# Pieces of the last layer's weight conversion tied to single chunks of the experts, and 20 instead of 16 of them in the last layer's first group

## The chip, the core and the metric

The kernel runs on one core of a Trainium2 chip. The core has five engines that run side by side and wait for each other by semaphores: PE (TensorE, matmuls; its weight loads are counted apart as PEld), DVE (VectorE), ACT (ScalarE), POOL (GpSimd) and SP (SyncE, which here only issues DMAs). Each engine takes its instructions strictly in the order in which they were put down for it. The metric is the device time of one execution in microseconds (us), lower is better. Before the change the median of 3 runs is 927.39 us (926.62 to 931.57).

## The reference: what is computed

Three layers one after the other, all in float32 at the outside.

```
attention:  state += beta * k_n (v - state k_n)^T,  y_t = q_t state     32 heads, 768 steps, 48 wide
experts:    logits = x w_gate + bias[modality];  e = argmax
            out = gate * (relu(x w1[e]) w2[e])                          3072 tokens, 384 -> 1024 -> 384, 8 experts
last layer: h = x w_in;  out = (h * sigmoid(h)) w_out                   3072 tokens, 384 -> 2048 -> 384
```

The weights `w_in` and `w_out` of the last layer come in as float64 (two 32-bit words per number). The kernel itself turns them into pairs of 32-bit numbers, a high part and a low part, since each product of the last layer is made of three matmuls: high by high, high by low, low by high. This conversion is what the change moves.

## The kernel before

**The experts.** Tokens are sorted by expert and handled in passes. The first five passes (0 to 4) take 2 blocks of 128 tokens each and overlap with the end of the attention layer and with the router, which works out on DVE where each token goes. Their order on every engine comes from a planner (class `Order`, `Experts.plan`), with a job for each step and a rank. Passes 0 to 2 use the weights as they are in the second product; passes 3 and 4 (`passes=(3, 4)`) split all weights into high and low parts. Then come four passes of 4 blocks each (`Experts.regular`, `Experts.slot`). Every pass goes through 8 chunks of the hidden width: `first` multiplies tokens by a chunk of w1 (9 matmuls, tile `ph` or `bank`), ACT makes the rectified high part and DVE the low part of the result (L1393 and L1397 into `hhl` in passes 3 and 4, L1474 and L1475 into `pairs` in the later ones), and `second` multiplies it by a chunk of w2 into `po` or `poe`. The high and low parts of the weights come from ACT (L1354, L1262) and DVE (L1357, L1263), out of buffers `raw` that SP fills by DMA. The 32 chunks of the four later passes are counted 40 to 71. In the last of these passes, after its first chunk, stands a test (`extra`, L1557 and L1558): every engine reads a number and branches around passes that are hardly ever needed.

**The conversion.** `Parts64` turns one part of the weights (12 parts `ri` of 128x512 of w_in, 16 parts `ro` of 128x384 of w_out). A part has a DMA, two DVE instructions that take bits out of the high words (L1586, L1587), one on ACT (L1588), then three on DVE (L1590, L1591, L1593), one on ACT that writes the high part (L1594) and one on DVE that writes the low part (L1595). `Ffn.chain` cuts the parts into pieces: piece 2i finishes part i (L1590 to L1595), piece 2i+1 asks for the load of part i+2 and begins part i+1 (L1586 to L1588). Two raw buffers are there, so a load of part i+2 waits until part i is read. The first 20 parts give 40 pieces that go with the experts, the last 8 parts (`ro8` to `ro15`) give 16 pieces that go with the first group of the last layer.

**What sets the order around the change.** The pieces are not jobs of the planner. They are traced in the loop over chunks 40 to 71, and a scheduler that simulates the program then puts every instruction in the place where it expects its operands. In the loop nothing ties a piece to its chunk, so a piece may be placed earlier than the chunk at which it was traced. In the last layer each piece is tied: `tc.issue_after(x)` puts what is traced under it behind instruction x, on x's engine.

**The last layer.** `Ffn.group` handles 512 tokens, in 16 steps f: `first(f)` (9 matmuls into `fph`, L1705), on ACT and DVE the activation and its high and low parts (L1708 to L1714), and `second(f-1)` into `fpo` (L1723). `tokens` loads the next group's tokens (`fy`) and transposes them on DVE.

Of the kernel before, what the change touches and what calls it, by code (L numbers as in the profile page):

```python
# [12 lines left out]
AF = mybir.ActivationFunctionType  # L13
ALU = mybir.AluOpType
# [12 lines left out]
        o=566.7, w=-158.5, wc=-114, up=-190.2, uc=85.6, ps=-63.1, sc2=420.4, py=136, Y=-126, out=290, xt=-319.5,  # L27
# [24 lines left out]
        xc2=-308.8, xc3=-299, xc4=-108.6, xc5=-186.8, gt0=-119.9, gt1=249, gt2=-393.6, gt3=-396.9, gt4=-275.9,  # L52
        gt5=-409.8,
    ), half=106.1,
    ex=-155.5, n0=40, npre=40, tok=70,
)


class Order:
# [137 lines left out]
    def emit(self, tc, pulse, close):  # L197

        nc = tc.nc
        traced, last = nc.cur_bb.bb.instructions, {}  # L200
        info = mybir.DependencyInfo(mybir.DependencyClass.NoSync, mybir.DependencyReason.DATA)
        wait = mybir.DependencyInfo(mybir.DependencyClass.Sync, mybir.DependencyReason.DATA)
        made = {}
        line = [(j["start"], 0, n, j) for n, j in enumerate(self.line)]
        final = max((x for x in line if x[3]["key"][0] not in self.LATER), key=lambda x: x[:3])[3]
        line += [(x, 1, n, k) for n, (x, k) in enumerate(self.pulses())]
        for _, kind, _, j in sorted(line, key=lambda x: x[:3]):
            at = len(traced)
            if kind:
                x = pulse()  # L210
                if j is not None:
                    tc.add_manual_dep(x, made[j], wait, reason="pulse")
            else:
                j["fn"]()
                if len(traced) > at:
                    made[j["key"]] = traced[-1].name
            new = {}
            for x in traced[at:]:
                new.setdefault(x.engine, []).append(x)
            for e, xs in new.items():  # L220
                for x in xs:
                    if e in last:
                        tc.add_manual_dep(x, last[e].name, info, reason="order")
                last[e] = xs[-1]
            if j is final:
                close()
# [10 lines left out]
class Attention:  # L237
# [501 lines left out]
    def run(self, router, experts, close):  # L739
        nc, P = self.nc, self.pools  # L740
        dense = router.ones
        room = self.ranks[:, 256:512].rearrange("p (a b) -> p a b", b=128)
        self.dense, self.rows = dense, [sized(x, [128, 16, 32]) for x in experts.po]

        def pulse():
            twice = [
                nc.tensor.matmul(room, dense, dense[:, None, :].to_broadcast([128, 2, 128]), start=True, stop=True).ins
                for _ in range(2)
            ]
            return twice[0]  # L750

        o = self.plan(router, experts)
        o.solve()
        o.emit(self.tc, pulse, close)


class Router:
# [454 lines left out]
class Experts:  # L1212
# [249 lines left out]
    def slot(self, n, blocks, x, po, fetch=None, nxt=None, last=False, alone=False, between=None):  # L1462

        nc, P, g, m = self.nc, self.P, self.r.groups[n], len(blocks)
        F, b0 = self.F, blocks[0]
        xh, xl = x

        def first(c, h1, l1):  # L1470
            ph = self.bank([128, 128 * m], f"ph{n}_{b0}_{c}")
            self.first(ph, h1, l1, xh, xl)
            hh, hl = self.take("hh", m), self.take("hl", m)
            nc.scalar.activation(hh, ph, AF.Relu)  # L1474
            nc.vector.scalar_tensor_tensor(hl, ph, 0.0, hh, op0=ALU.max, op1=ALU.subtract)  # L1475
            return hh, hl

        prev = None
        for c in range(F):
            w = self.split(0, c)  # L1480
            if between is not None and c == 1:
                between()
            cur = first(c, *w)
            w = self.split(1, c)
            if fetch is not None and c % 2:
                for part in range(2):
                    fetch(part, c - 1, c + 1)
            if prev is not None:
                self.second(c - 1, po, *prev)
            prev = cur + w  # L1490
            if alone:
                self.second(c, po, *prev)
                prev = None
            if nxt is not None:
                nxt(c)
            yield
        if prev is not None:
            self.second(F - 1, po, *prev)
        for t, o in enumerate(blocks):
            ysb = self.take("ysb", 4 * n)  # L1500
            if t % 2:
                nc.vector.tensor_scalar(ysb, po[t], g["gate"][:, o : o + 1], None, op0=ALU.mult)
            else:
                nc.scalar.mul(ysb, po[t], g["gate"][:, o : o + 1])
            self.scatter(n, o, ysb, last)
# [93 lines left out]
class Ffn:  # L1599
# [91 lines left out]
    def group(self, g, x, nxt, fill=()):  # L1691
        nc, P = self.nc, self.P
# [41 lines left out]
        prev = None  # L1734
        for f in range(16):
            cur = first(f)
            for fn in fill[f : f + 1]:
                with self.tc.issue_after(self.marks[0]), self.tc.issue_after(self.marks[1]):
                    fn()
            if f == 8 and nxt is not None:  # L1740
                self.x = self.tokens(nxt)
            if prev is not None and (f < 15 or nxt is not None):
                second(f - 1, *prev)
            if f < 15 or nxt is not None:
                prev = cur
# [71 lines left out]
@with_exitstack  # L1817
def fused_kernel(ctx: ExitStack, tc, kt, qb, kd, vd, beta, mod, w_gate, bias, w1, w2, w_in, w_out, out):
    nc = tc.nc

    def pool(stack, name, bufs=1, **kw):
        return stack.enter_context(tc.tile_pool(name=name, bufs=bufs, **kw))

    N, D = out.shape
    P = {
        "dram": pool(ctx, "dram", space=DRAM), "cc": pool(ctx, "cc"),
        "pa": pool(ctx, "pa", 5, space=PSUM), "pm": pool(ctx, "pm", 3, space=PSUM),
    }
    ident = P["cc"].tile([128, 128], F32, name="ident")

    xs = P["dram"].tile([N, D], F32, name="xs")
    ys = P["dram"].tile([N, D], F32, name="ys")
    P["rc"] = pool(ctx, "rc")

    with ExitStack() as moe:
        for name in ("ar", "ld"):
            P[name] = pool(moe, name, side="right")
        rank = ExitStack()
        P["rs"] = pool(rank, "rs", side="right")
        with ExitStack() as att:  # L1840
            for name in ("ac", "ln"):
                P[name] = pool(att, name)
            for name in ("sm", "y"):
                P[name] = pool(att, name, 2)
            attn = Attention(tc, ident, P, kt, qb, kd, vd, beta, xs)
            router = Router(tc, ident, P, attn.B, attn.T, w_gate, bias, mod, attn)
            experts = Experts(tc, ident, P, router, w1, w2, xs, ys, attn.bank)
            f = []

            def close():  # L1850
                att.close()
                P["fw"], P["f0"] = pool(ctx, "fw"), pool(ctx, "f0")
                f.append(Ffn(tc, ident, P, w_in, w_out, ys, out))
                add_pair_buffers(experts.bufs, P["fw"], f[0])
                P["rb"] = Views([P["fw"].tile([128, 6144], F32, tag=tag, name="scratch") for tag in ("il", "o0")])

            attn.run(router, experts, close)
        f = f[0]
        rank.close()
        raw = ctx.enter_context(ExitStack())  # L1860
        P["fr"] = pool(raw, "fr", 2)
        room = pool(raw, "fe")
        experts.bufs["ysb2"] = cut(room.tile([128, 1536], F32, name="ysb2"), [384] * 4)
        ws = cut(room.tile([128, 1536], F32R, name="w2s"), [384] * 4)
        experts.bufs["h2"], experts.bufs["l2"] = ws[0:2], ws[2:4]
        fill = f.chain(f.inner() + f.outer(range(0, 8), "o0"))
        n0, n1, at = PLAN["n0"], 9 * 8, 0
        for i, _ in enumerate(experts.regular(), n0):
            to = max(0, (i + 1 - n0) * PLAN["npre"] // (n1 - n0))
            for fn in fill[at:to]:  # L1870
                fn()
            at = max(at, to)
            if i == PLAN["tok"]:
                with tc.issue_after(experts.mark):
                    x0 = f.tokens(0)
        fill += f.chain(f.outer(range(8, 16), "o1"))

        def spare():
            raw.close()
            return pool(ctx, "fo", 2)  # L1880


        f.add(ffn_buffers(P["ar"]))
        f.run(x0, fill[at:], spare)
# [47 lines left out]
```

## Time and profile before

| | us |
|---|---|
| median of 3 runs (lowest, highest) | 927.39 (926.62, 931.57) |
| the execution in the profile | 931.44 |
| its span, first to last instruction | 929.7 |
| PE busy in the span | 884.8 |
| DVE busy in the span | 570.3 |
| ACT busy in the span | 425.0 |

The span is cut into stages by time. Attention, router and experts' passes overlap up to about 385 us; the four later passes run from there to about 518 us; the six groups of the last layer run from there to the end. Matmuls are pipelined, so a busy PE is not a PE at its peak. Idle time in the rows is the time in which an engine waited directly before an instruction, with the instruction that ended the wait behind the arrow.

### The profile page before, as it was taken

How to read it: one execution, taken by the hardware profiler on the slowest of the kernel's cores; microseconds unless marked ns; L12 is line 12 of the kernel's file. 1: busy time of each engine (PE TensorE's matmuls, PEld its weight loads, DVE VectorE, ACT ScalarE, POOL GpSimd, SP SyncE). 2: the span in 40 equal slices, each digit the busy share in tenths (PEclk: the TensorE clock that was granted, in tenths of full speed). 3: DMA queues.
4: the chain of work that ended last, by engine and by line, in shares of the span. 5: the costliest groups of instructions: out<-in, count | busy, mean ns of one | idle time of the engine just before them, and what ended most of it. 6: DMA issues, size and time to landing. Idle time of an engine off the chain costs nothing. (4 is left out here: it accounts for less than half of the span.)

```text
span 929.7 us, 23254 instructions
## 1 busy us (share of the span) xinstructions
PE 884.8 (95%) x9396; PEld 757.6 (81%) x9396; DVE 570.3 (61%) x1490; ACT 425.0 (46%) x838; POOL 154.1 (17%) x213
## 2 busy tenths in 40 slices
PE   7699999899999998999989999999999999999998
PEld 6488888798887687899878888888888888888887
DVE  4999789778614999998444576543443443443332
ACT  6046767477764456565434444332232233233232
POOL 4682008800010252122201100000000000000000
PEclk8798999799999999999998999999999999999999
DMA  9936657428426336766523431130130100100200
GB/s 190 170 83 135 164 132 186 105 66 246 112 45 195 109 108 192 230 197 204 168 65 72 89 88 35 15 54 1 18 51 1 22 14 1 26 8 1 31 6 34
DMA packets 135349, 85.25 MB, mean 92 GB/s; under 512 B 102361, under 2 KB 121447, under 8 KB 135232
## 3 DMA queue, kind: packets, MB, share of 16 engines
q1 hardware_dynamic: 131904, 73.84, 32.8%
q0 software_dynamic: 3328, 9.83, 3.4%
q8 instruction: 75, 1.23, 0.6%
q14 instruction: 42, 0.34, 0.1%
HBM read 70.53 MB, written 14.55 MB: 92 GB/s over the span
## 5 line engine op out<-in xcount | busy, mean ns | idle before, releaser
L1723 PE MATMUL fpo<-fgh,o 128*128 128x512 f32 x480 | 162.7, 396 | 0.0
L1710 DVE TENSOR_TENSOR fy<-fph,fy 128x512 f32<-128x512 f32 x96 | 66.3, 690 | 111.7 <-ACT fy L1708 111.3
L1714 DVE TENSOR_TENSOR fq<-fy,fgh 128x512 fp32r<-128x512 f32 x96 | 66.2, 689 | 108.7 <-ACT fgh L1712 101.2
L1712 ACT CAST fgh<-fy 128x512 fp32r<-128x512 f32 x96 | 59.6, 621 | 129.9 <-PE fpo L1723 98.7
L1708 ACT ACTIVATE fy<-fph 128x512 f32<-128x512 f32 x96 | 57.5, 599 | 126.6 <-PE fph L1705 124.5
L1705 PE MATMUL fph<-fxh,ih 128*128 128x512 f32 x288 | 113.5, 394 | 0.0
L1705 PE MATMUL fph<-fxh,il 128*128 128x512 f32 x288 | 113.4, 394 | 0.0
L1723 PEld LDWEIGHTS fpo<-fgh,o 128*128 128x128 f32 x480 | 90.3, 188 | 21.5
L1723 PE MATMUL fpo<-fq,o 128*128 128x512 f32 x240 | 95.1, 396 | 0.0
L1306 PE MATMUL poe<-w2s,pairs 128*128 128x384 f32 x384 | 75.5, 341 | 1.5 <-ACT pairs L1474 1.5
L1306 PEld LDWEIGHTS poe<-w2s,pairs 128*128 128x128 f32 x384 | 68.5, 190 | 4.9 <-ACT pairs L1474 1.8
L1705 PEld LDWEIGHTS fph<-fxh,ih 128*128 128x128 f32 x288 | 54.2, 188 | 12.3
L1705 PEld LDWEIGHTS fph<-fxh,il 128*128 128x128 f32 x288 | 54.2, 188 | 12.3
L1299 PE MATMUL bank<-xh,wRH 128*128 128x256 f32 x240 | 56.7, 313 | 3.4 <-DVE wRH L1357 3.1
L1705 PE MATMUL fph<-fq,ih 128*128 128x512 f32 x144 | 57.1, 396 | 0.0
L1705 PE MATMUL fph<-fxl,ih 128*128 128x512 f32 x144 | 56.4, 392 | 0.0
L1723 PEld LDWEIGHTS fpo<-fq,o 128*128 128x128 f32 x240 | 45.1, 188 | 10.8
L1267 POOL DMA_INDIRECT xg<-xs,gidx x26 | 30.8, 1183 | 127.5 <-PE bank L1281 89.5
L456 DVE TENSOR_TENSOR po<-po,tmp 128x126 f32<-128x126 f32 (+35 forms) x244 | 50.0, 250 | 0.1
L453 DVE TENSOR_TENSOR tmp<-po,L 128x126 f32<-128x126 f32 (+35 forms) x244 | 49.2, 242 | 0.7
L1299 PEld LDWEIGHTS bank<-xh,wRH 128*128 128x128 f32 x240 | 40.2, 192 | 9.7 <-DVE wRH L1357 4.2
L1299 PE MATMUL ph<-pairs,wRH 128*128 128x512 f32 x144 | 39.0, 411 | 3.7 <-DVEq L1558 3.7
(448 smaller groups left out, 1796.0 us busy)
## 6 DMA issues: line engine op xcount, KB each, us to landing
raw<-in_moe_w_dram SPq DMA_DIRECT2D x72, 384.0 KB
ri<-in_moe_w_in_dram SPq DMA_DIRECT2D x12, 512.0 KB
ro<-in_moe_w_out_dram SPq DMA_DIRECT2D x16, 384.0 KB
vs<-in_vd_dram SPq DMA_DIRECT2D x12, 384.0 KB
KI<-in_kd_dram SPq DMA_DIRECT2D x24, 192.0 KB
Z<-vs SPq DMA_DIRECT2D x24, 192.0 KB
xs<-Y SPq DMA_DIRECT2D x48, 96.0 KB
fy<-ys SPq DMA_DIRECT2D x72, 64.0 KB
```

The source lines that it names most:

```text
L453: eng.tensor_tensor(tv, row.to_broadcast([128, n, c]), l.to_broadcast([128, n, c]), op=ALU.mult)
L456: eng.tensor_tensor(x, x, tv, op=ALU.add)
L1267: self.nc.gpsimd.indirect_dma_start(out=rows, out_offset=None, in_=self.xs[0 : self.xs.shape[0] // (2 - n), :], in_offset=bass.IndirectOff ...
L1299: self.nc.tensor.matmul(ph, a[:, k, :], b[:, k, :], start=(i == 0), stop=(i == 8))
L1306: self.mark = self.nc.tensor.matmul(o, a[:, cs], b, start=(c == 0 and i == 0), stop=(c == self.F - 1 and i == 2)).ins
L1705: nc.tensor.matmul(ph, a[:, k, fs], b[:, k, :], start=(n == 0), stop=(n == 8))
L1708: nc.scalar.activation(sg, ph, AF.Sigmoid)
L1710: nc.vector.tensor_tensor(gv, ph, sg, op=ALU.mult)
L1712: self.marks = [nc.scalar.copy(gh, gv).ins]
L1714: self.marks.append(nc.vector.tensor_tensor(gl, gv, gh, op=ALU.subtract).ins)
L1723: nc.tensor.matmul(po[k], a[:, rows], b, start=(f == 0 and i == 0), stop=(f == 15 and i == 2))
```

## The change

The plan's numbers are `npre=36` instead of 40 and a new `test=(64, 65)`. So 36 pieces of the first 40 go with the experts, and the other 4 go in front of the 16 of the last layer's first group, which spreads 20 over its 16 steps. Of the 36, the first six are tied behind the rectified chunks 4 and 6 of pass 3 and 0, 2, 4 and 6 of pass 4; the other 30 are spread over the chunks 40 to 71 without 64, 65 and 71, and each is tied behind the rectified high part (on ACT) and low part (on DVE) of its chunk. To make this possible, the planner and the slots keep those two instructions as `marks`.

```
-    ex=-155.5, n0=40, npre=40, tok=70,
+    ex=-155.5, n0=40, npre=36, tok=70, test=(64, 65),
...
                     made[j["key"]] = traced[-1].name
+                    if j["key"][0] in ("rh", "rl"):
+                        self.marks[j["key"][:3]] = traced[-1]
...
-            nc.scalar.activation(hh, ph, AF.Relu)
-            nc.vector.scalar_tensor_tensor(hl, ph, 0.0, hh, op0=ALU.max, op1=ALU.subtract)
+            self.marks = [
+                nc.scalar.activation(hh, ph, AF.Relu).ins,
+                nc.vector.scalar_tensor_tensor(hl, ph, 0.0, hh, op0=ALU.max, op1=ALU.subtract).ins,
+            ]
...
-            for fn in fill[f : f + 1]:
+            for fn in fill[f * len(fill) // 16 : (f + 1) * len(fill) // 16]:
                 with self.tc.issue_after(self.marks[0]), self.tc.issue_after(self.marks[1]):
                     fn()
...
-        n0, n1, at = PLAN["n0"], 9 * 8, 0
+        early = [(3, 4), (3, 6), (4, 0), (4, 2), (4, 4), (4, 6)]
+        for fn, x in zip(fill, early):
+            with tc.issue_after(attn.marks["rh", *x]), tc.issue_after(attn.marks["rl", *x]):
+                fn()
+        n0, n1, at = PLAN["n0"], 9 * 8, len(early)
+        calm = [i for i in range(n0, n1 - 1) if i not in PLAN["test"]]
         for i, _ in enumerate(experts.regular(), n0):
-            to = max(0, (i + 1 - n0) * PLAN["npre"] // (n1 - n0))
+            past = sum(x <= i for x in calm)
+            to = len(early) + past * (PLAN["npre"] - len(early)) // len(calm)
             for fn in fill[at:to]:
-                fn()
-            at = max(at, to)
+                with tc.issue_after(experts.marks[0]), tc.issue_after(experts.marks[1]):
+                    fn()
+            at = to
```

The new lines shift the line numbers of the changed kernel: its L1592, L1593, L1596, L1597, L1599 and L1601 are the conversion's L1586, L1587, L1590, L1591, L1593 and L1595, its L1361 and L1401 are L1357 and L1397, its L1480 is L1475.

The first place is DVE in the router's sixth step, at about 295 to 300 us of the trace; L929 and L930 (`total`, `ca`) belong to the router, `wRH` is a split weight of the experts. Before:

```order
L927 TENSOR_TENSOR ca_5779<-cb_5776 128x16
L1586 TENSOR_SCALAR ri_0e<-ri_0_6579 128x512
L1587 TENSOR_SCALAR ri_0f<-ri_0_6579 128x512
L929 COPY total<-ca_5779 128x8
L1590 SCALAR_TENSOR_TENSOR ri_0f<-ri_0_6579,ri_0f 128x512
L930 TENSOR_TENSOR ca_5779<-ca_5779,OH 128x32
L1357 TENSOR_TENSOR wRH<-raw_4591,wRH 128x384 x2
L1591 SCALAR_TENSOR_TENSOR ri_0e<-ri_0_6579,ri_0e 128x512
L1586 TENSOR_SCALAR ri_1e<-ri_1_6581 128x512
```

And the same place in the changed kernel:

```order
L931 TENSOR_TENSOR ca_5779<-cb_5776 128x16
L933 COPY total<-ca_5779 128x8
L934 TENSOR_TENSOR ca_5779<-ca_5779,OH 128x32
L1361 TENSOR_TENSOR wRH<-raw_4591,wRH 128x384 x2
L948 TENSOR_TENSOR rk_5814<-ranks,OH 128x32
L950 TENSOR_REDUCE r_5_5816<-rk_5814 128x4
```

The conversion of the first two parts has left the router's steps; the router's and the experts' own instructions stand in the order that they had.

The second place is DVE in chunks 6 and 7 of pass 3, at about 352 to 356 us; `hhl` is the low part of a rectified chunk. Before:

```order
L1587 TENSOR_SCALAR ri_1f<-ri_1_6737 128x512
L1591 SCALAR_TENSOR_TENSOR ri_1e<-ri_1_6737,ri_1e 128x512
L1397 SCALAR_TENSOR_TENSOR hhl<-bank_124,hhl 128x256
L1357 TENSOR_TENSOR wRH<-raw_4591,wRH 128x384
L1357 TENSOR_TENSOR pairs<-raw_4700,pairs 128x384
L1591 SCALAR_TENSOR_TENSOR ri_2e<-ri_2_6831,ri_2e 128x512
L1587 TENSOR_SCALAR ri_2f<-ri_2_6831 128x512
L1590 SCALAR_TENSOR_TENSOR ri_1f<-ri_1_6737,ri_1f 128x512
L1397 SCALAR_TENSOR_TENSOR hhl<-bank_125,hhl 128x256
```

And in the changed kernel, from the same `hhl`:

```order
L1401 SCALAR_TENSOR_TENSOR hhl<-bank_124,hhl 128x256
L1592 TENSOR_SCALAR ri_1e<-ri_1_6543 128x512
L1593 TENSOR_SCALAR ri_1f<-ri_1_6543 128x512
L1361 TENSOR_TENSOR wRH<-raw_4591,wRH 128x384
L1361 TENSOR_TENSOR pairs<-raw_4700,pairs 128x384
L1601 TENSOR_TENSOR il<-ri_0f,ih 128x512
L1401 SCALAR_TENSOR_TENSOR hhl<-bank_125,hhl 128x256
L1361 TENSOR_TENSOR wRH<-raw_4591,wRH 128x384
```

Between one `hhl` and the next now stands one piece or none, of part 0 or part 1 of w_in, where it was two parts at a time, parts 4 and 5.

The third place is DVE at the end of the last pass of the experts, at about 511 to 520 us. Before, no conversion stood here:

```order
L1688 TENSOR_TENSOR fxl<-fpt_2_12083,fxh 128x512
L1263 TENSOR_TENSOR w2s<-raw_4700,w2s 128x384
L1475 SCALAR_TENSOR_TENSOR pairs<-ph_12_6_12032,pairs 128x512
L1263 TENSOR_TENSOR w2s<-raw_4700,w2s 128x384
L1475 SCALAR_TENSOR_TENSOR pairs<-ph_12_7_12089,pairs 128x512
```

And in the changed kernel:

```order
L1694 TENSOR_TENSOR fxl<-fpt_2_12073,fxh 128x512
L1267 TENSOR_TENSOR w2s<-raw_4700,w2s 128x384
L1480 SCALAR_TENSOR_TENSOR pairs<-ph_12_6_12015,pairs 128x512
L1596 SCALAR_TENSOR_TENSOR ro5f<-ro_11938,ro5f 128x384
L1592 TENSOR_SCALAR ro6e<-ro_12006 128x384
L1593 TENSOR_SCALAR ro6f<-ro_12006 128x384
L1597 SCALAR_TENSOR_TENSOR ro5e<-ro_11938,ro5e 128x384
L1599 SCALAR_TENSOR_TENSOR ro5f<-ro5f,ro5e 128x384
L1480 SCALAR_TENSOR_TENSOR pairs<-ph_12_7_12079,pairs 128x512
```

Between the low parts of the last two chunks now stand five instructions of the parts 5 and 6 of w_out, one of which needs the load of part 6. On SP the loads of the parts moved with their pieces; those of `ro5`, `ro6` and `ro7` now stand among the loads of `fy`, the last layer's tokens.

## Rows read from the trace of the kernel before

**Rows 1.** The page's first part: busy time of each engine, share, instructions.

```profile
PE 884.8 (95%) x9396; PEld 757.6 (81%) x9396; DVE 570.3 (61%) x1490; ACT 425.0 (46%) x838; POOL 154.1 (17%) x213
```

**Rows 2.** Waits of PE from 290 to 930 us: total us, times, longest.

```profile
PE ph L1299 <- DVEq L1558: 3.7, 1, 3.7
PE bank L1299 <- DVE wRH L1357: 3.1, 4, 1.1
PE po L1306 <- DVE hhl L1397: 2.3, 5, 0.9
PE ranks L936 <- DVE ca L930: 2.0, 1, 2.0
PE poe L1306 <- ACT pairs L1474: 1.5, 1, 1.5
PE ranks L747 <- DVE scratch L1152: 0.9, 1, 0.9
PE po L1306 <- ACT hhl L1393: 0.2, 1, 0.2
```

**Rows 3.** Timeline of PE: start, us, instruction; idle before and its releaser.

```profile
298.36 0.18 PE L936 MATMUL ranks<-ca,ones 128*128 128x32 bf16 x1 [1.95 <-DVE ca L930]
...
381.38 1.66 PE L1306 MATMUL poe<-w2s,pairs 128*128 128x384 f32 x8 [1.46 <-ACT pairs L1474]
...
488.00 4.21 PE L1299 MATMUL ph<-pairs,wRH 128*128 128x512 f32 x9 [3.72 <-DVEq L1558]
```

**Rows 4.** Timeline of DVE, 296 to 301 us, the same columns.

```profile
296.73 0.43 DVE L1586 TENSOR_SCALAR ri_0e<-ri 128x512 int32<-128x512 int32 x1 [1.69 <-DMA ri<-in_moe_w_in_dram]
...
297.41 0.16 DVE L929 COPY total<-ca 128x8 bf16<-128x8 bf16 x1
...
298.14 0.17 DVE L930 TENSOR_TENSOR ca<-ca,OH 128x32 bf16<-128x32 bf16 x1
...
299.16 0.68 DVE L1591 SCALAR_TENSOR_TENSOR ri_0e<-ri,ri_0e 128x512 int32<-128x512 int32 x1
299.77 0.42 DVE L1586 TENSOR_SCALAR ri_1e<-ri 128x512 int32<-128x512 int32 x1
300.10 0.42 DVE L1587 TENSOR_SCALAR ri_1f<-ri 128x512 int32<-128x512 int32 x1
```

**Rows 5.** Stretches: length, busy us of each engine, PE's granted clock, DMA.

```profile
290.00:296.00 6.00, 6.00 (x39) 4.53 (x32) 2.55 (x14) 2.00 (x7) 0.00 (x0) 1.00 0.69 228
298.40:302.30 3.90, 3.90 (x15) 2.97 (x14) 3.59 (x10) 1.51 (x4) 0.00 (x0) 0.56 0.48 154
302.30:340.00 37.70, 34.53 (x229) 27.76 (x228) 36.34 (x99) 16.67 (x40) 10.86 (x8) 1.00 0.25 80
340.00:385.00 45.00, 40.15 (x251) 36.12 (x251) 45.00 (x97) 30.59 (x68) 14.52 (x10) 1.00 0.69 221
385.00:435.00 50.00, 50.00 (x257) 45.08 (x256) 46.91 (x101) 30.29 (x62) 11.23 (x8) 1.00 0.64 203
435.00:482.00 47.00, 47.00 (x248) 42.73 (x247) 23.45 (x43) 19.71 (x41) 8.86 (x9) 1.00 0.43 131
482.00:492.00 10.00, 6.28 (x22) 5.09 (x21) 2.86 (x5) 2.76 (x6) 2.22 (x3) 0.72 0.14 47
518.00:593.00 75.00, 75.00 (x331) 61.51 (x330) 49.17 (x94) 33.64 (x58) 4.92 (x4) 1.00 0.26 59
```

**Rows 6.** Stretches for line L1590 alone: length, its DVE busy us and count.

```profile
296.00:340.00 44.00, 1.38 (x2) 0.96 0.30 100
340.00:385.00 45.00, 5.38 (x8) 1.00 0.69 221
```

**Rows 7.** Timeline of ACT, 379 to 382 us.

```profile
379.80 1.05 ACT L1411 ACTIVATE raw<-po,gate 128x384 f32<-128x384 f32 x2
380.73 1.08 ACT L1474 ACTIVATE pairs<-ph 128x512 fp32r<-128x512 f32 x2
```

**Rows 8.** Timeline of DVE, 428 us: the longest wait for a part's load after 385 us.

```profile
428.83 0.36 DVE L1586 TENSOR_SCALAR ro7e<-ro 128x384 int32<-128x384 int32 x1 [1.24 <-DMA ro<-in_moe_w_out_dram]
```

More of the change, by code (lines that the diff above doesn't have):

```diff
@@ L203, in emit @@
         made = {}
+        self.marks = {}
         line = [(j["start"], 0, n, j) for n, j in enumerate(self.line)]
@@ L754, in run @@
         o.emit(self.tc, pulse, close)
+        self.marks = o.marks
 class Router:
```

## The prediction

> **What bounds the kernel now.** The page's busy times come first: PE is busy for 884.8 of 929.7 us, DVE for 570.3 [rows 1]. So the end moves only if PE's idle time or its slow time gets less. The waits of PE show where it stands still from 290 us on [rows 2]: seven kinds, 13.7 us together. One is the test in the last pass of the experts (3.7 us). The other six sum to 10.0 us, and the timeline of PE places the first of them at 298.36 us and the last at 381.38 us [rows 3]. The table of stretches says the same from the other side: PE is busy for all of 385 to 482 us and of 518 to 593 us, but for 34.53 of 37.70 us before 340 and 40.15 of 45.00 us from 340 to 385 [rows 5]. In these two stretches DVE is busy for 36.34 and 45.00 us: DVE is the bound there, and four of the six kinds (3.1, 2.3, 2.0 and 0.9 us) name it. What the change does to DVE between 296 and 385 us is therefore the question, and whether the later stages can take the work.
>
> **What leaves DVE between 296 and 385 us.** Line L1590 ran 10 times there [rows 6]. L1591, L1593 and L1595 go with it once per part (10 each), L1586 and L1587 are one part ahead (11 each): 40 long and 22 short instructions. From start to start a long one takes 299.77 - 299.16 = 0.61 us, a short one 300.10 - 299.77 = 0.33 us [rows 4]: 40 x 0.61 + 22 x 0.33 = 31.7 us, of the 36.34 + 45.00 = 81.3 us that DVE works there. In the changed order three parts and the beginning of a fourth are left ahead of the four later passes, 12 long and 8 short: 10.0 us. So 21.7 us go, over a quarter of DVE's work in the stage.
>
> **Term 1: the stop at 298.36 us.** PE waits 1.95 us for the router's L930 [rows 3]. DVE itself had waited 1.69 us for the load of the first part, whose L1586 stood ahead of L929 and L930, and spent another 297.41 - 296.73 = 0.68 us on it and 0.6 us between them [rows 4]. In the changed order nothing of the conversion stands there, and L930 would be done about 3 us earlier, before PE asks. That gives 1.95 us. [...] The bounds are 1.9 us (the clock falls at another place) and 3.7 us. I take 3.1, between them and nearer the upper end, since the 1.69 us is the landing of one load in one execution.
>
> **Term 2: the waits for split weights, low parts and the router's scratch.** These are 3.1 + 2.3 + 0.9 us, and 0.2 us for ACT's `hhl` [rows 2], 6.5 us in all. They come from instructions that queue behind others on DVE. With a quarter of the queue gone most should go; not all, because the router's own long instructions still stand ahead of split weights. Bounds: 0 and 6.5. I take 5.0, by the rows that are nearest: from 385 to 435 us DVE is busy for 46.91 of 50.00 us, nearly as much as before 385, and PE does not stop once [rows 5]; the new load, (81.3 - 21.7) of 82.7 us, is 72%.
>
> **Term 3: the stop at 381.38 us.** PE waits 1.46 us for ACT's L1474, which stands on ACT behind two evictions of `po` of 1.05 us [rows 3, 7]. In the changed order the evictions still stand ahead of it and PE's `poe` still comes right after the last `po`. I take 0; bounds 0 and 1.5.
>
> **Term 4: what comes in later.** Behind 385 us there is one piece per chunk, where 20 pieces stood before between 385 and 435 us. A piece is half a part, (4 x 0.61 + 2 x 0.33) / 2 = 1.6 us of DVE. From 435 to 482 us DVE works 23.45 of 47.00 us [rows 5]; the 11 chunks there add about 17 us and give 41 of 47, less than the 46.91 of 50.00 that stopped PE for nothing. In the last layer's first group 4 pieces more (6 us) make 55 of 75 us. So the cover is PE's own stream, and it holds as long as DVE's instructions come in time. It can fail where a piece stands at the head of DVE's queue and its load has not landed: the longest such wait after 385 us was 1.24 us [rows 8], and PE did not stop for it. The loads moved on SP too: those of `ro5` to `ro7` stand among the loads of `fy`, and the one of `ro6` must wait until `fy` has been transposed. What is queued behind it on DVE is the low part of the experts' last chunk, and PE waits for that; PE has two steps of the last layer to do first. I take 0.7 us for this, with bounds 0 and 1.24 x 4 = 5.0, if four parts around the start of the last layer come late and nothing covers them.
>
> **Edits at nothing.** The test costs 3.7 us and a clock of 0.72 over 482 to 492 us [rows 2, 5]; it stands at the same place on PE, and the two short instructions (0.66 us) that now stand ahead of it on DVE fall in time in which DVE works 2.86 of 10 us. Everything from about 600 us on is the same work in the same stream.
>
> **The sum.** 3.1 + 5.0 + 0 - 0.7 = 7.4 us off the profiled execution's 931.44 us (span 929.7), so 924.0 for that one. It was 4.05 us above the median of the runs; nothing in it says that the excess lies in these stops, beyond what I took off term 1. From the median, 927.39 - 7.4 = 920.0 us. With the bounds of all terms the gain lies between 1.9 - 5.0 = -3.1 and 11.7 us.
>
> [...] From 302.3 to 340 us PE is busy for 34.53 us, 3.1 us short, but its weight loads only for 27.76 of 37.70 us, a share of 0.74; from 385 to 435 us it is 45.08 of 50.00, or 0.90 [rows 5]. [...]
>
> **Rivals.**
> [...] Chance 0.10.
>
> Half the gain: the stops are only shared out anew. The queue in front of the router's long instructions is shorter, but PE comes sooner as well, meets the next late instruction on DVE or the raw weights' loads, and term 2 gives 1.5 instead of 5.0: 927.39 - 3.9 = 923.5. Or the median runs never had the late load of 298 us, and term 1 gives 0 there: 923.1. For it speaks that the runs differ by 4.95 us among themselves; against it that DVE is not merely full but names four of the six waits. Chance 0.22. That the change does nothing is the end of this case: the order has moved, so DVE's work does leave the stage, but PE might be held by something else that the profile puts down to DVE; 927.4.
>
> Slower: the piece now stands right behind the low part of its chunk and ahead of the split weights and the next low part, in each of some 28 chunks from 385 us on. If each meets PE as `hhl` did, 2.3 / 5 = 0.46 us a time [rows 2], that is 12.9 us, and 920.0 + 0.7 + 12.9 = 933.6 us. It decides from 0.29 us per chunk on, where 28 of them eat the 8.1 us of terms 1 and 2. Against it speaks 385 to 435 us, where 20 pieces did PE no harm [rows 5]; for it, that there the scheduler was free to place each instruction and now it is not. Chance 0.10.
>
> **How the numbers follow.** The forecast, 920.0 us, has 0.58, with its own range of 917 to 922.7; more 0.10 (914.5 to 917); half or nothing 0.22 (922 to 927.5); slower 0.10 (928 to 936). To hold 8 in 10 the range goes from 915 to 927: it leaves out the slower case and a little at each end. A run of this kernel can be told from no change at about 0.5%, or 4.6 us: faster is below 922.75, slower above 932.0. Below 922.75 lie nearly all of the forecast, the 0.10 of more and a small part of half: 0.56 + 0.10 + 0.03 = 0.69. Above 932.0 lies 0.07. The rest, 0.24, is the same.
>
> **What would show it.** In the profile after: no wait of PE for L930's successor near 297 us and a clock of 1.00 in the 4 us behind it; `hhl` and `wRH` waits that sum to under 2 us instead of 5.4; a wait of about 1.5 us for L1474's successor at the first `poe`; PE busy without a gap between there and the test; DVE at some 85% after 435 us where it was at 50%. The forecast is wrong if PE shows waits on DVE in the four later passes or at the start of the last layer, if the waits before 385 us stay with other releasers (raw loads, ACT), or if the clock falls at a new place.

## The result

The changed kernel takes 914.82 us (median of 4 runs, 913.11 to 920.41); the kernel before, timed beside it, 927.0 us (4 runs, 925.77 to 931.57). The ratio is 0.9882 with a 95% interval of 0.9846 to 0.9917, so 11 us less; on the 927.39 us of the forecast it makes 916.4. A second timing of the same pair gave 0.9852 (0.9808 to 0.9895). The forecast was 920.0, with a range of 915 to 927: right in sign and in its main cause, its gain too small by 3.6 us by the ratio. The median itself lies 0.2 us under the range.

### The profile page after: what moved, and what is told of

Same layout as the page of the kernel before. It is cut to its first block, busy times and chain, and to the rows that moved or that the text cites. A ratio compares the mean times of both kernels' runs of the same rounds, so it can differ in the third digit from the quotient of the medians.

```text
span 911.4 us, 23258 instructions
## 1 busy us (share of the span) xinstructions
PE 873.0 (96%) x9396; PEld 749.3 (82%) x9396; DVE 570.8 (63%) x1490; ACT 424.7 (47%) x838; POOL 145.5 (16%) x213
## 5 line engine op out<-in xcount | busy, mean ns | idle before, releaser
L1729 PEld LDWEIGHTS fpo<-fq,o 128*128 128x128 f32 x240 | 45.1, 188 | 10.8
L1271 POOL DMA_INDIRECT xg<-xs,gidx x26 | 27.5, 1059 | 130.3 <-PE bank L1285 86.7
```

Of the source, the lines that this page charges most:

```text
L1271: self.nc.gpsimd.indirect_dma_start(out=rows, out_offset=None, in_=self.xs[0 : self.xs.shape[0] // (2 - n), :], in_offset=bass.IndirectOff ...
L1729: nc.tensor.matmul(po[k], a[:, rows], b, start=(f == 0 and i == 0), stop=(f == 15 and i == 2))
```

## The profile after, and where the time went

First the page's busy times of the changed kernel (span 911.4 us, profiled execution 913.11), which answer to [rows 1]. PE lost 11.8 us of busy time as well as idle time (7.30 us of it ahead of the router, by the tables below); DVE does the same work.

```profile
PE 873.0 (96%) x9396; PEld 749.3 (82%) x9396; DVE 570.8 (63%) x1490; ACT 424.7 (47%) x838; POOL 145.5 (16%) x213
```

The waits of PE from 285 us on (total, times, longest), which answer to [rows 2]: 7.6 us in four kinds instead of 13.7 in seven. The waits for `hhl` and for the router's `ca` are gone; the test and the first `poe` are as they were.

```profile
PE ph L1303 <- DVEq L1564: 3.8, 1, 3.8
PE bank L1303 <- DVE wRH L1361: 1.7, 2, 1.1
PE poe L1310 <- ACT pairs L1479: 1.5, 1, 1.5
PE ranks L750 <- DVE scratch L1156: 0.6, 1, 0.6
```

To split the 18.3 us between the two spans, take the same PE instruction in both traces: the router's last count (`ranks<-OH,tri`, 296.23 us before and 288.59 after), a matmul of a split weight (`bank<-xh,wRH`) behind the stop at `ca` (302.29 and 290.80), the first `poe` of the later passes (381.38 and 363.01) and the first `fph` of the last layer (517.86 and 499.70). Table of stretches of the kernel before, between these points, and a short one (76 to 90.5 us) that is used with e11 (length, busy us of PE, PEld, DVE, ACT and POOL with counts, granted clock, DMA share, GB/s):

```profile
0.00:296.23 296.23, 269.65 (x6457) 238.56 (x6458) 215.66 (x821) 176.57 (x371) 99.75 (x171) 0.93 0.59 140
...
76.00:90.50 14.50, 13.57 (x347) 12.98 (x343) 14.26 (x75) 8.83 (x20) 0.95 (x1) 0.76 0.59 129
...
296.23:381.38 85.15, 75.19 (x474) 63.77 (x472) 82.97 (x202) 47.79 (x108) 23.83 (x17) 0.98 0.49 155
302.29:381.38 79.09, 71.08 (x460) 60.68 (x458) 77.73 (x188) 45.57 (x104) 23.83 (x17) 1.00 0.48 151
381.38:517.86 136.48, 132.76 (x667) 119.48 (x668) 90.21 (x178) 64.59 (x131) 25.58 (x22) 0.97 0.50 144
```

The same stretches of the changed kernel, and then those that answer to [rows 5] from 385 us on:

```profile
0.00:288.59 288.59, 262.35 (x6457) 231.40 (x6458) 216.45 (x825) 176.81 (x371) 99.43 (x171) 0.95 0.60 143
288.59:363.01 74.42, 70.66 (x475) 62.53 (x473) 64.86 (x164) 41.00 (x97) 19.29 (x17) 1.00 0.45 143
290.80:363.01 72.21, 68.45 (x461) 60.73 (x459) 62.83 (x158) 40.26 (x96) 19.29 (x17) 1.00 0.43 137
363.01:499.70 136.69, 132.90 (x666) 119.60 (x667) 103.07 (x201) 69.02 (x138) 22.23 (x22) 0.98 0.53 155
...
367.00:417.00 50.00, 50.00 (x256) 45.10 (x255) 40.19 (x75) 26.75 (x54) 9.27 (x9) 1.00 0.55 175
417.00:464.00 47.00, 47.00 (x248) 42.70 (x248) 36.95 (x76) 25.13 (x53) 8.46 (x8) 1.00 0.57 177
464.00:474.00 10.00, 6.21 (x23) 5.01 (x22) 2.86 (x5) 3.12 (x7) 2.33 (x3) 0.72 0.13 46
500.00:575.00 75.00, 75.00 (x331) 61.65 (x330) 53.98 (x105) 35.35 (x62) 4.58 (x4) 1.00 0.31 75
```

The stretch from the router's last count to the first `poe`, called the router stretch from here on, is 10.73 us shorter (85.15 to 74.42). Behind it nothing is lost: 136.48 and 136.69 us to the first `fph`, and 406.37 and 406.24 from there to the last matmul. The other 7.64 us lie ahead of the router, where the instructions are the same (DVE has got four further ones done by then, two of the router and two split weights); e11 below shows that one kernel differs by more than that between two executions, so they are not put down to the change.

## The experiments

All diffs are against the changed kernel. The ratio to the kernel before has its 95% interval. Router stretch and DVE's and PE's busy time in it are from each one's own profile; "ahead" is the number of conversion instructions that DVE's order has ahead of the first low part of the later passes.

| kernel | ahead | DVE busy | PE busy | router stretch | first `poe` to `fph` | ratio |
|---|---|---|---|---|---|---|
| before | 57 | 82.97 | 75.19 | 85.15 | 136.48 | 1 |
| e11 (before again) | 57 | 82.89 | 74.76 | 84.18 | 136.91 | |
| e1 | 57 | 82.45 | 74.50 | 87.04 | 136.52 | 1.0011 (0.997 to 1.0052) |
| e2 | 57 | 81.78 | 75.23 | 86.37 | 140.44 | 1.003 (0.9991 to 1.0068) |
| e3 | 49 | 77.93 | 72.63 | 79.74 | 136.84 | 0.9951 (0.9909 to 0.9994) |
| changed | 20 | 64.86 | 70.66 | 74.42 | 136.69 | 0.9882 (0.9846 to 0.9917) |
| e9 (changed again) | 20 | 64.98 | 70.36 | 73.01 | 137.12 | 0.9852 (0.9808 to 0.9895) |
| e7 | 20 | 64.80 | 70.61 | 73.92 | 137.53 | 0.9877 (0.9809 to 0.9944) |
| e8 | 20 | 64.84 | 70.67 | 74.42 | 136.43 | 0.9877 (0.9806 to 0.9948) |
| e4 | 0 | 56.11 | 70.21 | 71.60 | 136.21 | 0.9842 (0.9804 to 0.988) |
| e10 (e4 again) | 0 | 56.72 | 69.81 | 71.15 | 137.03 | 0.9854 (0.9809 to 0.9899) |
| e5 | 0 | 56.07 | 69.89 | 71.22 | 136.62 | 0.9848 (0.9786 to 0.9911) |
| e6 | 0 | 55.96 | 70.11 | 71.46 | 136.84 | 0.9842 (0.978 to 0.9905) |

**e1: only the first stop.** The late pieces are free again, as before the change (36 and 20 of them stay); the first one stands behind the router's last subtraction.

```diff
-            nc.vector.tensor_tensor(c, c, OH, op=ALU.subtract)
+            self.sub = nc.vector.tensor_tensor(c, c, OH, op=ALU.subtract).ins
...
-        early = [(3, 4), (3, 6), (4, 0), (4, 2), (4, 4), (4, 6)]
+        early = [0]
...
-            with tc.issue_after(attn.marks["rh", *x]), tc.issue_after(attn.marks["rl", *x]):
+            with tc.issue_after(router.sub):
...
-                with tc.issue_after(experts.marks[0]), tc.issue_after(experts.marks[1]):
-                    fn()
+                fn()
```

> As the kernel before (no piece is tied to a chunk), but the first piece of the conversion is queued on DVE behind the router's last subtraction into ca instead of ahead of it; 16 + 4 pieces in the last layer's first group. Measured by the stretch from the router's last count (ranks<-OH,tri) to the first poe of the later passes: 85.15 us before, 74.42 after the change. Theory A (the stop of 298 us is one late instruction of the router behind a waiting load): the stop and the slow clock behind it go, 3.85 us, everything else stays: 81.3 us, total 0.996 of before. Rival B (the wait for the load only moves on to the split weights and rk that now stand behind the part): PE stops there instead, the stretch is 84 to 85 us, total 0.999 to 1.000.

The stop at `ca` is gone, and a longer one has come. It ends 14.0 us behind the router's last count, where the stop at `ca` ended 2.1 us behind it. DVE's timeline of e1 (start, us, instruction, idle before and its releaser): it waits for three loads, the third right ahead of the router's 3.35 us instruction, and behind that stands the split weight that PE needs.

```profile
289.96 0.43 DVE L1592 TENSOR_SCALAR ri_0e<-ri 128x512 int32<-128x512 int32 x1 [0.55 <-DMA ri<-in_moe_w_in_dram]
...
292.40 0.43 DVE L1592 TENSOR_SCALAR ri_1e<-ri 128x512 int32<-128x512 int32 x1 [1.12 <-DMA ri<-in_moe_w_in_dram]
...
299.47 0.43 DVE L1592 TENSOR_SCALAR ri_2e<-ri 128x512 int32<-128x512 int32 x1 [2.07 <-DMA ri<-in_moe_w_in_dram]
299.81 3.35 DVE L1044 TENSOR_TENSOR scratch<-lane,pm 128x3072 bf16<-128x3072 f32 x1
303.08 0.55 DVE L1361 TENSOR_TENSOR wRH<-raw,wRH 128x384 fp32r<-128x384 f32 x1
```

PE's timeline, and the stretch behind the stop:

```profile
303.69 0.80 PE L1303 MATMUL bank<-xh,wRH 128*128 128x256 f32 x2 [6.66 <-DVE wRH L1361]
```

```profile
303.69:307.50 3.81, 3.81 (x17) 3.81 (x18) 3.75 (x15) 1.41 (x3) 0.35 (x1) 0.50 0.46 151
```

The stretch is 87.04 us, 1.9 longer than before. Theory A is wrong; B's kind of thing happened, and more of it. DVE is busy for as long as before (82.45 us), and waits for loads for 3.74 us where it waited for 1.95 (1.69 and 0.26). Taking one stop away without taking work off DVE moved the stop.

**e2: the first piece later, everything else free.**

```diff
-        early = [(3, 4), (3, 6), (4, 0), (4, 2), (4, 4), (4, 6)]
+        early = [(3, 0)]
...
-                with tc.issue_after(experts.marks[0]), tc.issue_after(experts.marks[1]):
-                    fn()
+                fn()
```

> As the kernel before, but the first piece is tied behind the first chunk of the fourth early pass; all other pieces are free. 57 conversion instructions still run on DVE ahead of the later passes, as many as before (20 after the change), but none of them ahead of about 318 us of before. Theory A (what counts is the amount of conversion that DVE has in this stage): only the stop of 298 us goes, and the same work in less time keeps the other stops: stretch 80 to 82 us, total 0.995 to 0.997. Rival B (what counts is which instructions it stands ahead of, the split weights of 304 to 320 us above all): the three stops there go as well, 2.2 us of idle time: stretch 77.5 to 78.5 us, total 0.992.

The stops of 304 to 320 us did go, but PE stood still for 2.98 and 2.17 us at 327 and 334 us and for 3.03 us at the first `poe`; DVE had waited 2.63 us for one load ahead of the second of these; what released the first the profile does not show. The stretch is 86.37 us, so both theories missed. B is out: the stops only went elsewhere. A has the amount right (DVE is busy for 81.78 us, within 1.2 us of before) and its figure of 80 to 82 us wrong, since it took off the price of a stop that comes back in another place. Behind the first `poe` e2 lost another 3.96 us: the clock was 0.56 for 3.9 us, PE stopped once more for 1.38 us, and the stop at the test took 4.26 us.

```profile
331.96 0.43 DVE L1592 TENSOR_SCALAR ri_0e<-ri 128x512 int32<-128x512 int32 x1 [2.63 <-DMA ri<-in_moe_w_in_dram]
```

```profile
327.28 1.05 PE L1310 MATMUL po<-pairs,hhl 128*128 128x384 f32 x4 [2.98 <-issue]
333.70 0.98 PE L1310 MATMUL po<-pairs,hhl 128*128 128x384 f32 x4 [2.17 <-DVE pairs L1361]
...
375.60 2.77 PE L1310 MATMUL poe<-w2s,pairs 128*128 128x384 f32 x8 [3.03 <-ACT pairs L1479]
```

**e3: 16 pieces early, one behind each chunk.**

```diff
-        early = [(3, 4), (3, 6), (4, 0), (4, 2), (4, 4), (4, 6)]
+        early = [(s, c) for s in (3, 4) for c in range(8)]
```

> The changed kernel with 16 pieces instead of 6 tied to chunks of the last two early passes, one per chunk; the other 20 of the 36 are spread over the later passes. 49 conversion instructions run ahead of the later passes, against 20 in the changed kernel and 57 before. Theory A (amount on DVE): by a straight line between 20 at 74.42 us and 57 at 81.3 us (before without the stop of 298 us) the stretch is 79.8 us, total 0.994. Rival B (order, not amount: one piece behind each chunk's low part stops nothing): 74.5 to 76 us, total 0.988 to 0.990.

The stretch is 79.74 us. Rival B is out: no piece stands ahead of the router's chain here, and DVE waits for no load; still PE stops nine times, the first `poe` among them, for up to 1.52 us. That theory A said 79.8 us is partly luck: its line starts at 81.3 us for 57 instructions, and e1 and e2, with 57, had 87.04 and 86.37; from the 85.15 us of before the line gives 82.8. What fits is DVE's own time: it is busy for 5.04 us less than before, and the stretch is 5.41 us shorter. In e1 and e2, where the stretch is 4.6 us longer than DVE's busy time, DVE waited for loads for 3.74 and 2.96 us.

**e4: none early.**

```diff
-        early = [(3, 4), (3, 6), (4, 0), (4, 2), (4, 4), (4, 6)]
+        early = []
```

> The changed kernel with no piece ahead of the later passes: all 36 are tied to their 29 chunks. Theory A (amount on DVE): the waits for split weights and scratch that the changed kernel still has there (1.12, 0.61 and 0.57 us) go, with some 0.3 us of restart each: stretch 71 to 72 us; DVE in the later passes goes from 77 to some 86 of 97 us and still hides it; total 0.985. Rival B (those waits are the router's own long instructions): the stretch stays at 74.4 us, total 0.988. Rival C (the pieces behind the marks fill DVE in the later passes and PE waits for low parts and for the last layer's first steps): up to 5 us more behind the first poe, total 0.990 to 0.994.

Theory A holds in both halves. The stretch is 71.60 us, and both waits for split weights are gone; the wait for scratch (0.58 us) stays, so that one is the router's own. From the first `poe` to 458 us PE does not stop, with DVE busy for 86.59 of 96.57 us (86 of 97 was expected). Table of stretches of e4, the router stretch and the later passes up to 458 us:

```profile
289.83:361.43 71.60, 70.21 (x474) 62.49 (x472) 56.11 (x143) 36.84 (x89) 17.68 (x17) 1.00 0.39 126
...
361.43:458.00 96.57, 96.57 (x502) 87.74 (x503) 86.59 (x169) 56.46 (x111) 19.42 (x18) 1.00 0.63 197
```

**e5: as e4, only the first piece tied.** e4's edit, and

```diff
-                with tc.issue_after(experts.marks[0]), tc.issue_after(experts.marks[1]):
-                    fn()
+                if fn is fill[0]:
+                    with tc.issue_after(experts.marks[0]), tc.issue_after(experts.marks[1]):
+                        fn()
+                else:
+                    fn()
```

> As e4 (no conversion ahead of the later passes), but only the first piece is tied to its chunk; the other 35 are free once their data allow it. By the order 85 of 108 conversion instructions then run in the first 20 chunks of the later passes, against 71 in e4: about 43 us of conversion beside some 22 us of other DVE work in 67 us. Theory A (the ties matter only because they keep DVE free ahead of the first poe): the stretch from the router's last count to the first poe is 71 to 72 us as in e4 (71.60), and the time from the first poe to the first fph stays at 136 to 137 us: total 0.984 of before. Rival B (free pieces crowd the low parts and the ties are needed there too): PE stops behind the first poe, 138 to 141 us there, total 0.987 to 0.990.

71.22 and 136.62 us, theory A. PE stops once for 0.59 us in the later passes. So the other 35 ties are worth little by themselves, and one tie, of the first piece, is enough to keep all pieces out of the router stretch.

**e6: as e4 with 40 pieces ahead of the last layer.** e4's edit, and `npre=40`.

> As e4, but 40 instead of 36 pieces in the later passes and so 16 instead of 20 in the last layer's first group. DVE is busy for 86.6 of 96.6 us behind the first poe in e4; four pieces of 1.4 us more make 92 of 97 us. Theory A (PE stops only when DVE has no slack left): still no stop, stretch 71.6 us, first poe to first fph 136.2 us, total 0.984. Rival B (near the limit single instructions come late): stops of some 0.3 to 0.9 us each, 1 to 4 us in all behind the first poe, total 0.986 to 0.989.

No new stop before the test, though the stretch of 136.84 us has 116.73 us of DVE. But the test takes 4.80 us (below). The time is 0.9842 of before, as in e4.

**e7: 16 pieces in the last layer.** The changed kernel with `npre=40`.

> The changed kernel with 40 pieces ahead of the last layer and 16 in its first group, as before the change; the six early ones stay. Theory A (four pieces more or less in the last layer are hidden behind PE): all three stretches as in the changed kernel: 74.4 us, 136.7 us, and 406.2 us from the first fph to the last matmul; total 0.988. Rival B (the last layer pays for 20 pieces): its first group is shorter by 0.5 us or more, total 0.987.

The last layer takes 406.35 us against 406.24: 16 or 20 there is all one. The router stretch has one stop less (73.92 us). What changes is the test, 4.94 us. PE's timeline at the test, in e6, in e7 and in e8:

```profile
471.39 3.91 PE L1303 MATMUL ph<-pairs,wRH 128*128 128x512 f32 x9 [4.80 <-DVEq L1564]
```

```profile
468.78 4.21 PE L1303 MATMUL ph<-pairs,wRH 128*128 128x512 f32 x9 [4.94 <-DVEq L1564]
```

```profile
474.22 3.84 PE L1303 MATMUL ph<-pairs,wRH 128*128 128x512 f32 x9 [3.91 <-DVEq L1564]
```

In ten other profiles the stop is 3.63 to 3.91 us, in e2 4.26. With 40 tied pieces ahead of the last layer it is 1 us longer in both kernels; that is what 20 instead of 16 pieces in the last layer brings. The number alone does not do it: the kernel before has 40 ahead as well, free ones, and 3.72 us. That the last instruction of a part stands right ahead of the test on DVE in both is the likely reason; no run here isolates it.

**e8: pieces at the test too.** The changed kernel with `test=()`.

> The changed kernel with pieces tied to chunks 64 and 65 too, the two ahead of the test in the last pass. Theory A (the test waits for something else than DVE's queue): the stop of PE at the test stays at 3.8 us, total 0.988. Rival B (DVE reaches the test later by the pieces that stand ahead of it, 1.4 us each): the stop grows to 5 to 6.5 us, total 0.989 to 0.991.

3.91 us, theory A; the changed kernel has 3.79 us, and 3.63 in e9, so leaving chunks 64 and 65 out is worth 0.3 us at most.

**e9 and e10: the changed kernel and e4 side by side**, with no edit.

> The changed kernel unaltered, beside the next one on one chip. Theory A (10.7 us come from the stretch between the router's last count and the first poe, the rest of the 18.3 us between the two profiles is where the clock happened to fall in the first 100 us): the stretch is 74.4 us again, total 0.988 of before, 11 us. Rival B (the change also shortens the stages ahead of the router): total 0.982 or less, 16 us and more.

> e4 once more (no piece ahead of the later passes, 36 tied to their chunks). Theory A: stretch 71.6 us and 136.2 us behind it, so 3.3 us less than the changed kernel: total 0.9845 of before, some 0.0035 below e9. Rival B (the difference between e4 and the changed kernel was one execution's): within 1 us of e9.

The stretches came near theory A's 74.4 and 71.6 us (73.01 and 71.15), but the totals did not tell the two apart, as rival B of e10 has it: 0.9852 and 0.9854. e4 is 1.9 to 2.8 us shorter in the router stretch; the time ahead of the router differs by more than that from run to run. So e4 is not shown to be faster than the changed kernel.

**e11: the kernel before, profiled again**, with no edit.

> The kernel before, unaltered, profiled a second time. Theory A (the stop of 298 us belongs to the order, and the time ahead of the router does not): the router's last count starts 3 to 9 us earlier than the 296.23 us of the first profile, as in the ten kernels since (285.98 to 292.95 us), and the stretch from there to the first poe is 84 to 87 us again with the clock below 1.00 behind the stop at ca. Rival B (the load of the first part was late by chance): no stop at ca, stretch 81 to 82 us.

Theory A in the main: the router's last count starts at 285.87 us, 10.36 us earlier than in the first profile of the very same kernel (3 to 9 were expected), and the router stretch is 84.18 us. Its table of stretches has the time ahead of the router (the same counts of instructions on every engine as in the first profile, clock 0.96 instead of 0.93), 76 to 90.5 us (444 matmuls at 1.00 instead of 347 at 0.76), the two parts of the router stretch, and the time behind PE's second stop; then comes PE's timeline:

```profile
0.00:285.87 285.87, 261.43 (x6457) 230.78 (x6458) 215.74 (x821) 176.78 (x371) 99.48 (x171) 0.96 0.61 145
...
76.00:90.50 14.50, 14.50 (x444) 13.62 (x441) 14.23 (x83) 11.95 (x28) 0.32 (x1) 1.00 0.60 134
...
285.87:289.92 4.05, 2.59 (x17) 1.94 (x15) 4.04 (x12) 1.46 (x4) 0.00 (x0) 1.00 0.51 178
289.92:370.05 80.13, 72.17 (x460) 61.68 (x459) 78.85 (x191) 46.24 (x106) 24.99 (x17) 0.98 0.47 155
...
297.20:301.00 3.80, 3.80 (x18) 3.30 (x19) 3.77 (x15) 2.04 (x5) 1.47 (x2) 0.66 0.49 128
```

```profile
287.51 0.18 PE L936 MATMUL ranks<-ca,ones 128*128 128x32 bf16 x1 [1.46 <-DVE ca L930]
...
289.92 0.58 PE L1299 MATMUL bank<-xh,wRH 128*128 128x256 f32 x1
...
297.20 0.50 PE L1299 MATMUL bank<-xh,wRH 128*128 128x256 f32 x2 [2.17 <-DVE wRH L1357]
```

The stop at `ca` is there again (1.46 us), without a slow clock behind it; the slow clock came behind the next stop of 2.17 us. The stops inside the stretch are shared out anew from run to run, and its length stays within 1 us: 85.15 and 84.18 us.

## Why the prediction was right, and where it was too small

**DVE bounds the stage before 385 us: right.** DVE is busy for 82.97 of 85.15 us of the router stretch. With 49 or 57 conversion instructions the stretch is DVE's busy time plus 1.3 to 4.6 us. With 20 or fewer it is PE's 70 to 71 us plus the waits that are left, and DVE, busy for 56 to 65 us, counts only through these. What leaves DVE was put too high: 21.7 us, counted to 385 us. Up to the first `poe` 37 conversion instructions and 82.97 - 64.86 = 18.11 us left, and since the stretch got shorter too, DVE is busy for 87% of it and not for 72%.

**Term 1 (3.1 us): size near, step wrong.** Between the router's last count and 302.29 us the kernel lost 6.06 - 2.21 = 3.85 us: 1.95 of idle time, and 1.90 in which PE was busy for longer with the same matmuls, 4.11 instead of 2.21 us (75.19 - 71.08 and 70.66 - 68.45), at a granted clock of 0.72 instead of 1.00. That is above the step's upper bound of 3.7 us. But the step took the stop as a thing of its own, one late load ahead of L930. e1 put L930 ahead of the load and got a stop of 6.66 us; e11 had 1.46 us there and no slow clock. In e11 the same two parts of the stretch take 4.05 and 80.13 us, so against the changed kernel the two terms would be 1.84 and 7.92 us there: one execution's split, of which only the sum holds. What the upper bound, and with it the 3.1 us, holds beyond the stop itself was the author's estimate from the clock of 0.56 in [rows 5]; no run shows that term by itself. In its place the runs showed the 1.90 us here and 4.05 - 1.46 - 2.21 = 0.38 us in e11. The 3.85 us are a part of DVE's overload, and in no run were they saved without work leaving DVE.

**Term 2 (5.0 us, bound 6.5): mis-sized, this is where the forecast fell short.** It measured 79.09 - 72.21 = 6.88 us. PE's idle time in it fell from 8.01 to 3.76 us, 4.25 less, near the forecast. The other 2.63 us were busy time of PE: 71.08 to 68.45 us at a clock of 1.00, for the same matmuls and the same time of weight loads (60.68 and 60.73). A stop here cost more than the idle time that the view of waits puts down to it. Over the router stretches at a clock of 1.00, PE is busy for 69.89 us with one stop inside (e5; 69.81 to 70.21 in the four profiles with one), 70.67 with three (e8) and 72.63 with eight (e3), so 0.39 us per stop: (72.63 - 69.89) / 7. The rows around one stop of the kernel before show the greater part of it:

```profile
349.69 0.28 PE L1299 MATMUL bank<-xh,wRH 128*128 128x256 f32 x1
349.81 0.28 PE L1299 MATMUL bank<-xl,wRH 128*128 128x256 f32 x1
350.96 0.50 PE L1299 MATMUL bank<-xh,wRH 128*128 128x256 f32 x2 [0.88 <-DVE wRH L1357]
...
351.42 0.40 PE L1299 MATMUL bank<-xh,wRH 128*128 128x256 f32 x2
```

Matmuls here start 0.12 us after each other (349.69 to 349.81) and overlap. The last one ahead of the stop counts as busy for all of its 0.28 us, 0.16 us more; the two behind it take 0.50 us where the next two take 0.40. Together that is 0.26 us. Matched with e4 matmul by matmul, ten of the eleven stops of term 2 show 0.25 to 0.27 us; at the eleventh, for the router's scratch, e4 stops as well. The rest of the 0.39 us lies at late starts for which the view shows no idle time, so 0.39 is the upper figure. With 0.26 to 0.39 us a stop, the upper bound of term 2, with its eleven stops, was 9.4 to 10.8 us (6.5 + 11 x 0.26 and 6.5 + 11 x 0.39) and not 6.5.

**Term 3 (0): right.** The stop at the first `poe` is 1.46 us in both. It falls to 0.76 or 0.77 us where no conversion is left ahead of it (e4 to e6), so about half of it hung on the conversion ahead of it, and not on the two evictions alone.

**Term 4 (-0.7 us): right, a little too dear.** The stretch behind the first `poe` lost 0.21 us, the last layer nothing. DVE waits there for no load of a part, and PE is busy for 50.00 of 50.00 and 47.00 of 47.00 us, as forecast, with DVE at 79% (85% was expected).

**The sum**: 0.75 (term 1) + 1.88 (term 2) + 0.6 (term 4) is what the 7.4 us lacked against 10.7.

**The rivals.** "More" (chance 0.10, 914.5 to 917) has the measured time in its range. The stretch before 340 us, where PE's busy time was 3.1 us short, gave 37.30 - 33.66 = 3.64 us; in e4, with 0.58 us of stops left in it, it took 33.65 us. Its share of weight loads rose from 0.74 to 0.82, not to the 0.90 of 385 to 435 us, which is another stage with other matmuls. What came beyond the forecast is in terms 1, 2 and 4 above. "Half the gain" had a true part, that stops are only shared out anew, and e1 and e2 show it, with DVE busy for 82.45 of 87.04 us and for 81.78 of 86.37; it did not hold where DVE was busy for 56 to 65 us. "Slower" has nothing: not one wait of PE for a low part in the four later passes.

The first profile of before was 4 us above the median; the forecast left open whether the stops held that excess. Between the two profiles of before, 931.44 and 920.50 us, 10.36 us of the difference lie ahead of the router and 0.97 in the router stretch; so such a spread does not come from the stops. The profile after lay 1.7 us below its median.

## What to carry to other kernels

Where an engine other than PE is busy for 97% of a stage, as DVE was in this one, do not price PE's stops one by one: here they moved from place to place, from run to run and from edit to edit. Take the stage as the longer of that engine's work and of PE's work at full clock without stops, and ask how much work has to leave until the second is the longer; past that point more relief bought little here (20 to 0 instructions: 1.9 to 2.8 us; 57 to 20: 11). In this stage a stop cost PE 0.26 to 0.39 us beyond its idle time, so several small ones are dearer than the view of waits says.

## What was not expected of the hardware

The same instructions in the same order took from 285.87 to 296.23 us up to the router, in two executions of one kernel; between 76 and 90.5 us the granted clock was 1.00 in one and 0.76 in the other. That spread is as large as the change's effect, which is why this account goes by stretches and not by spans.

Behind six stops of PE in the router stretch or at its end (1.95 us in before, 2.17 in e11, 2.17, 2.98 and 3.03 in e2, 6.66 in e1) the clock was between 0.50 and 0.66 for the next 3.7 to 3.9 us; behind stops of 1.46 us in before, e3 and e11 it stayed at 1.00. The rows of e2, then that of before and that of e3 (that of before for 1.95 us is in [rows 5], those of e1 and e11 stand above):

```profile
327.28:331.00 3.72, 3.72 (x17) 3.68 (x18) 2.05 (x6) 1.60 (x4) 0.36 (x1) 0.60 0.78 247
333.70:337.50 3.80, 3.80 (x19) 3.76 (x20) 3.80 (x9) 1.38 (x4) 0.24 (x1) 0.65 0.03 5
375.60:379.50 3.90, 3.90 (x12) 3.67 (x13) 3.90 (x8) 1.80 (x4) 0.63 (x1) 0.56 0.89 274
...
381.38:385.00 3.62, 3.62 (x18) 3.21 (x19) 3.62 (x8) 1.70 (x4) 1.55 (x1) 1.00 0.84 279
...
337.35:341.00 3.65, 3.65 (x26) 3.58 (x26) 3.65 (x8) 2.31 (x6) 0.00 (x0) 1.00 0.08 30
```
